# Sums of weights moved from GpSimd to VectorE, relu and square of h moved to ScalarE in two tiles, and one continued schedule

## The chip, the cores and the metric

The kernel runs on one core of a Trainium2 chip. The metric is the device time of that core in microseconds. Before the change the median of three runs is 893.88 us (890.68 to 894.46).

A core has five engines that run side by side, each through its own queue of instructions in order: TensorE (PE in the profile; PEld is its weight loads), VectorE (DVE), ScalarE (ACT), GpSimd (POOL) and SyncE (SP), which here issues nearly all DMAs. An instruction that waits holds back everything behind it on its engine.

## The reference

Attention without a softmax over scores, and then a two-layer network on its output:

```python
q_s = exp(q - max(q, axis=-1)); q_s /= sum(q_s, axis=-1) + 1e-9      # over the 64 features
k_s = exp(k - max(k, axis=2));  k_s /= sum(k_s, axis=2) + 1e-9       # over the 576 positions
kv  = einsum('bhsd,bhse->bhde', k_s, v)
x   = einsum('bhsd,bhde->bhse', q_s, kv)      # (8, 8, 576, 64) -> 4608 rows of 512
h   = maximum(x @ w_in, 0)                    # w_in 512 x 2048
out = (h * h) @ w_out                         # w_out 2048 x 512
```

q, k and v have 8 batches, 8 heads, 576 positions and 64 features, all in float32.

## The kernel before, in words

**Tiles.** A tile is the first 512 rows of one batch (t = 0 to 7), and a ninth tile holds the last 64 rows of all eight batches. While the network of tile t runs on PE, the attention of batch t + 1 runs beside it, in four pairs of heads; its result is the next tile's input `x`. The network goes by 16 blocks f of 128 hidden columns: `first` makes `h` of block f in a PSUM bank (two banks, tag "h", take turns) by 12 products, `split_g` turns it into its square, and `second` adds the square's products with w_out to four accumulators, for block f - 2. Each float32 operand is held as a high part and a rest (`gh` and `gl` for the square, `hi` and `lo` elsewhere), and three of the four cross products are taken.

**Relu and square.** ScalarE makes `r` = relu(h). For f under `ON_ACT` (14) VectorE then makes h = max(h, 0) * r in the bank itself (`scalar_tensor_tensor`), ScalarE makes `gh` = r squared, and VectorE `gl` = h - gh, which is the bank's last reader. For f from 14 on, in t = 1 and 2, ScalarE squares `r` in place, and the bank is free after the relu.

**Sums of weights.** Tiles t = 3 to 5 and the closing stage multiply by a Strassen-Winograd scheme: 7 products of half-size blocks take the place of 8, and they need sums of blocks of the weights (s1 to s4). `in_sums` prepares those of w_in in t = 1 and 2 (8 keys, in three steps), `full_sums`, `add_sums`, `split_sums`, `rest_sums` and `keep_sums` those of w_out in t = 3 to 6 (7 keys; an eighth is made in the closing stage). Each key adds the high parts and rests to full weights, makes four sums of 256 columns, has ScalarE copy them to a high part (`sums_h`), subtracts that from them in place, and sends both to memory. Before the change nearly all of this but the copy is GpSimd's; one of the two full additions of a w_in key is VectorE's. Buffers are few: pool `cvt` has two of tag "w", which the sums share with the output tiles `o`.

**GpSimd's other work.** From t = 1 on it is one `partition_all_reduce` for each pair of heads (`k_reduce`): the maximum of k over the 128 partitions, from `km` to `kmx`. The compiled program has a row ISA without operands where GpSimd goes over from ordinary additions to an all-reduce and one where it comes back.

**Order.** `Planner` sets the order of all engines at once. `Engine` gives each call a duration (`base + per * n` us, for VectorE 0.14 + 0.00108 * n, n being the columns), `order` places calls one after the other at the earliest free time of their engine, by the longest remaining chain (`tail`), and `plan.due` ties a call to a block of the network. The program has two plans: one for t = 0 (`plan.run`) and one for t = 1 to 5 (`plan.run_on`). Between them x is split and tile 0 is closed (`split_x`, `end_tile`, `prepare`) in the order of the code, and `reopen` then starts the second plan from an empty chip, every engine free at time zero. Tile 6 and the closing stage are in the order of the code. Nothing in the planner's durations stands for what GpSimd does between an addition and an all-reduce.

Of the kernel before, what the change touches and what calls it, by code (L numbers as in the profile page):

```python
# [132 lines left out]
class Planner:  # L133
# [9 lines left out]
    def __init__(self):  # L143
        self.open, self.nodes, self.into, self.chain, self.boot = True, [], None, None, []
        self.marks, self.line = {}, {}
        self.due, self.dues = None, []
        self.ease = 0.0
        self.locked, self.slack = False, 1.0

    def reopen(self, pools):  # L150

        for n in self.nodes:
            for b in n.buffers:
                b.seen, b.users, b.choices = [], [], ()
                b.last = b.before = b.placed = None
        for p in pools:
            p.told.clear()
        self.__init__()
        self.line, self.locked, self.slack, self.ISSUE = None, True, 1.06, 0.8

    def run_on(self):

# [122 lines left out]
            n.tail -= n.ease  # L285
    def order(self):

        left = {n: len(n.before) for n in self.nodes}
        for n in self.nodes:
            n.since, n.start, n.end = 0.0, None, None  # L290
            for b in n.buffers:
                b.placed = None
        ready = [n for n in self.nodes if not left[n]]
        free, dma, told, port = {}, self.FIRST, [], 0.0
        self.banks = {}
        while ready:
            able = []
            for n in ready:
                t = max(free.get(n.engine, 0.0), n.since)
                if self.locked and n.port:  # L300
                    t = max(t, port)
                if n.behind is not None:
                    if n.behind.start is None:
                        continue
                    t = max(t, n.behind.start + n.behind.busy)
                for b in n.buffers:
                    if b.placed is not None:
                        continue
                    at, _ = self.place(b)
                    if at is None:  # L310
                        break
                    t = max(t, at + self.HOP)
                else:
                    able.append((t, n))
            t0, n0 = min(able, key=lambda x: x[0])
            t, n = max(
                ((t, n) for t, n in able if n.engine is n0.engine and t <= t0 + self.WAIT),
                key=lambda x: x[1].tail,
            )
            n.start, n.end = t, t + n.busy  # L320
            free[n.engine] = n.end
            if n.port:
                port = n.end
            if n.moved:
                dma = max(dma, n.end) + n.moved / self.RATE
                n.end = dma + self.LAND
            for b in n.buffers:
                if b.placed is None:
                    b.placed = t
                    if b.choices:  # L330
                        b.pool, b.tag = self.place(b)[1]
                        self.banks[b.tag] = float("inf")
            for b in n.buffers:
                if b.choices and all(u.end is not None for u in b.users):
                    self.banks[b.tag] = max(u.end for u in b.users)
            told.append(n)
            ready.remove(n)
            for o in n.after:
                left[o] -= 1
                o.since = max(  # L340
                    o.since, n.end + (0.0 if o.engine is n.engine and not n.moved else self.HOP)
                )
                if not left[o]:
                    ready.append(o)
        return told

    def shift(self, seed):
# [23 lines left out]
def attention_ffn(  # L371
# [30 lines left out]
    C = 4  # L402
# [33 lines left out]
    WT = B - 1  # L436
    STRASSEN = range(3, WT - 1)
    DUE = 3
    ON_ACT = 14
    assert B * TL == M and DM == NP * P and C * P == M  # L440

    def pool(name, bufs, to=ctx, **more):
# [727 lines left out]
    def in_sums(j, i):  # L1170

        key = "in", j
        if i == 0:
            full = made["full", key] = cvt.tile([P, 2, M], F32, tag="w", name=f"full_i{j}")
            for k in range(2):
                slab = slabs[2 * j + k]
                (V if k else G).tensor_tensor(
                    out=full[:, k, :].only(k), in0=slab[:, 0, :], in1=slab[:, 1, :], op=ALU.add,
                    n=M if k else 575,
                )  # L1180
        elif i == 1:
            full = made.pop(("full", key))
# [8 lines left out]
            for out, in0, in1, op in (  # L1191
                (s1, a21, a22, ALU.add), (s2, s1, a11, ALU.subtract),
                (s3, a11, a21, ALU.subtract), (s4, a12, s2, ALU.subtract),
            ):
                G.tensor_tensor(out=out, in0=in0, in1=in1, op=op, n=260)
            hi = cvt.tile([P, 2, 2, HM], F32R, tag="w", name=f"sums_h_i{j}")
            for k in range(2):
                S.copy(out=hi[:, k].only(k), in_=two[k])
# [1 line left out]
        else:  # L1200
            hi, two = made.pop(("split", key))
            for k, (at, by) in enumerate(((4, 2), (8, 4))):
                to = w_sums[j][:, at:at + 2 * by, :].rearrange("p (n t) c -> p n t c", t=by)
                names = ("s2", "s1") if k == 0 else ("s3", "s4")
                lo = two[k].bitcast(F32R)
                G.tensor_tensor(out=lo, in0=two[k], in1=hi[:, k].only(k), op=ALU.subtract, n=575)
                for m, part in enumerate((hi[:, k].only(k), lo)):
                    Y.dma_start(
                        out=to[:, :, m, :].only(*((name, m) for name in names)),
                        in_=part.bitcast(F32), kb=256,  # L1210
                    )
# [106 lines left out]
    def store(t, acc, c):  # L1318
# [9 lines left out]
        if t == 0:  # L1328
            rows = rows.rearrange("(d a b c) e -> c d b a e", c=C, a=2, b=32)[c]
            for d in range(2):  # L1330
                Y.dma_start(out=rows[d], in_=o[d * HD:(d + 1) * HD, :])
        elif t < TB:
            rows = rows.rearrange("(h p k) e -> h k p e", h=2, k=2)[c % 2, c // 2]
            Y.dma_start(out=rows, in_=o, kb=256)
# [190 lines left out]
    def end_tile(t, parts, acc, one, two):  # L1525

        for c, f in (
            (0, one), (1, one), (0, two), (1, two), (2, one), (2, two), (3, one), (3, two),
        ):
            second(t, f, parts[f], acc, c, end=two)  # L1530
            if f == two:
                store(t, acc, c)

    KEYS = [("o", j) for j in range(PAIRS - 1)]
    IN_SUMS = [(j, i) for j in range(PAIRS) for i in range(3)]

    def sums_step(t, f):
# [5 lines left out]
                in_sums(*IN_SUMS.pop(0))  # L1543
        for key, at in SUMS_AT.get(t, ()):
            if f == at[0]:
                full_sums(key, 0, G)
            if f == at[1]:
                full_sums(key, 1, G)
            if f == at[2]:
                for n in range(3):  # L1550
                    add_sums(key, n, G)
            if f == at[3]:
                add_sums(key, 3, G)
                split_sums(key)
            if f == at[4]:
                rest_sums(key, G)
            if f == at[5]:
                keep_sums(key)

# [258 lines left out]
    for t in range(WT):  # L1818
        if t == 1:
            for i in range(NF):  # L1820
# [1 line left out]
                    whole[i] = whole[i].only((key, i, 0), (key, i, 1))  # L1822
                wi_h[i], wi_l[i] = (slabs[i][:, m, :].only(("i", i, m)) for m in range(2))
                wo_h[i], wo_l[i] = (slabs_o[i][:, m, :].only(("o", i, m)) for m in range(2))
            plan.reopen((const, att, cvt, ffn, tiny, boot, late, ps_o, ps_h, ps_a, dram))
        x_next = begin_next(t)
        if t in STRASSEN:
            acc = None
# [54 lines left out]
                ahead(f, x_next)  # L1883
        if t == 0:
            plan.run(SEEDS, fill)
            x = split_x(x_next, t + 1)
            end_tile(t, parts, acc, NF - 2, NF - 1)
            if todo[-1][1] == NF - 1 and t + 2 < B:
# [379 lines left out]
```

## Time and profile before

| | |
|---|---|
| median of three runs | 893.88 us (890.68 to 894.46) |
| profiled execution | 894.29 us, of it span 892.5 us |
| PE busy | 823.4 us (92% of the span), 4941 products |
| VectorE, ScalarE, GpSimd busy | 563.7, 451.3, 238.5 us |
| chain that ended last | PE 67%, DMA 12%, issue 9%, DVE 4%, POOL 3%, ACT 3% |
| mean granted TensorE clock | 0.973 |

PE is the engine with the most work, and its end is the kernel's. Stretches of the span used below: t = 1 from 133 to 237 us, t = 2 to 344, t = 3 to 5 to 641, t = 6 to 745, then the closing stage. To read the profile, ask of a stretch how long PE was idle, what released it, and at what clock it went on: a granted clock of 1.00 is 2.4 GHz, 0.50 is 1.2 GHz. The busy time of PE is not all useful time, since at the lower clock the same products count for longer. GpSimd's "issue" is idle time in which it waited for nothing that the profile shows.

### The profile page before, as it was taken

The numbers are of one execution on the slowest core, as the hardware profiler recorded it, in microseconds if no ns is written. First come the engines' busy times: TensorE is split into PE (matmuls) and PEld (weight loads), VectorE is DVE, ScalarE is ACT, GpSimd is POOL, SyncE is SP. The second block draws the span as 40 slices with busy tenths as digits, with TensorE's granted clock in tenths as the row PEclk, the third lists the DMA queues.
The fourth block names the chain that finished last, engine by engine and source line by source line (L and its number), as shares of the span: only waits on it lengthen the run. The fifth ranks groups of instructions, "written<-read, shape, count | busy, mean of one in ns | idle before, by whom it ended". The sixth has DMA issues, their size and how long they took to land.

```text
span 892.5 us, 14319 instructions
## 1 busy us (share of the span) xinstructions
PE 823.4 (92%) x4941; PEld 699.0 (78%) x4941; DVE 563.7 (63%) x1107; ACT 451.3 (51%) x864; POOL 238.5 (27%) x257
## 2 busy tenths in 40 slices
PE   8989998869997999898999799499998999999997
PEld 6678876748786877787888788388886888888886
DVE  6988976446583657465766566365675763327895
ACT  5888753233442335555666456255633344557452
POOL 4899953350024230412022302222021000000000
PEclk9999999989998999999999999799999999999999
DMA  9991126557232337986988779498944316999675
GB/s 282 385 338 39 48 49 177 162 178 216 56 109 62 107 105 206 262 259 189 250 250 243 217 211 287 133 259 241 275 122 118 86 39 226 377 374 343 231 204 95
DMA packets 224903, 174.28 MB, mean 195 GB/s; under 512 B 133568, under 2 KB 193472, under 8 KB 224832
## 3 DMA queue, kind: packets, MB, share of 16 engines
q1 hardware_dynamic: 218912, 171.67, 63.6%
q10 hardware_dynamic: 5920, 1.71, 0.8%
q8 instruction: 39, 0.64, 0.3%
q14 instruction: 32, 0.26, 0.1%
HBM read 129.37 MB, written 43.38 MB: 194 GB/s over the span
## 4 chain that ended last, share of the span: by engine, by line
PE 67%; DMA 12%; issue 9%; DVE 4%; POOL 3%; ACT 3%; SPq 2%; POOLq 0%; ACTq 0%; DVEq 0%
PE h L101 23%; PE acc L101 22%; PE out L2042 8%; PE h L1311 8%; PE kv L101 4%; DMA ring<-w_sums 3%; DMA bst<-bst 2%; SPq L101 2%; DMA q<-in_q_dram 2%; POOL sums_i L101 1%; DMA raw<-in_moe_w_out_dram 1%; DMA k<-in_k_dram 1%; DMA raw<-in_moe_w_in_dram 1%; DVE bst L101 1%; POOL sums_o L101 1%
## 5 line engine op out<-in xcount | busy, mean ns | idle before, releaser
L101 PE MATMUL acc<-w,gh 128*128 128x512 f32 x888 | 270.2, 386 | 2.7 <-DVE g L101 1.8
L101 PE MATMUL h<-x,w 128*128 128x512 f32 x768 | 190.0, 398 | 22.6 <-DVE gl L101 21.5
L101 PEld LDWEIGHTS h<-x,w 128*128 128x128 f32 x768 | 148.4, 197 | 53.6 <-DVE gl L101 24.6
L101 PEld LDWEIGHTS acc<-w,gh 128*128 128x128 f32 x888 | 159.9, 191 | 29.2 <-issue 6.7
L101 PE MATMUL acc<-w,gl 128*128 128x512 f32 x444 | 169.2, 381 | 0.7 <-DVE gl L101 0.7
L101 PEld LDWEIGHTS h<-w,ring 128*128 128x128 f32 x720 | 92.2, 192 | 24.5 <-ACT u L101 15.5
L101 PE MATMUL h<-w,ring 128*128 128x256 f32 x720 | 94.5, 278 | 17.4 <-ACT u L101 14.7
L101 POOL PARTITION_ALL_REDUCE kmx<-km x24 | 18.2, 760 | 289.7 <-DVE km L101 229.0
L101 PEld LDWEIGHTS acc<-w,gl 128*128 128x128 f32 x444 | 84.5, 190 | 14.0 <-DVE gl L101 1.9
L101 ACT ACTIVATE c<-c 128x512 f32<-128x512 f32 (+1 forms) x134 | 79.4, 592 | 19.1 <-DVE c L101 17.2
L2042 PE MATMUL out<-w,w 128*128 128x512 f32 x324 | 72.2, 379 | 0.0
L2042 PEld LDWEIGHTS out<-w,w 128*128 128x128 f32 x324 | 61.2, 189 | 8.8
L101 DVE TENSOR_TENSOR gl<-h,gh 128x512 fp32r<-128x512 f32 x59 | 40.4, 685 | 42.0 <-ACT gh L101 40.3
L101 ACT ACTIVATE r<-h 128x512 f32<-128x512 f32 x64 | 37.8, 590 | 47.0 <-PE h L101 47.0
L101 DVE SCALAR_TENSOR_TENSOR h<-h,r 128x512 f32<-128x512 f32 x60 | 41.5, 692 | 28.9 <-ACT r L101 28.6
L101 ACT ACTIVATE gh<-r 128x512 fp32r<-128x512 f32 x63 | 39.6, 629 | 39.5 <-PE acc L101 38.8
L101 ACT COPY u<-h 128x256 f32<-128x256 f32 x72 | 26.7, 371 | 52.3 <-PE h L101 52.0
L101 DVE TENSOR_REDUCE bst<-q 128x18 f32<-128x576 f32 x48 | 35.9, 748 | 25.9 <-DMA q<-in_q_dram 20.5
L101 DVE TENSOR_TENSOR c<-h,u 128x256 f32<-128x256 f32 x72 | 29.8, 418 | 34.3 <-ACT u L101 17.6
L101 PE MATMUL h<-w,w 128*128 128x256 f32 x288 | 39.5, 288 | 10.1 <-ACT u L101 6.8
L101 PEld LDWEIGHTS h<-w,w 128*128 128x128 f32 x288 | 37.8, 201 | 13.8 <-ACT u L101 8.2
L101 DVE TENSOR_TENSOR bst<-bst 128x18 f32<-128x18 f32 (+1 forms) x96 | 25.0, 260 | 33.6 <-DMA bst<-bst 18.6
(191 smaller groups left out, 1256.2 us busy)
## 6 DMA issues: line engine op xcount, KB each, us to landing
ring<-w_sums SPq DMA_DIRECT2D x24, 768.0 KB, 6.0
ring<-w_sums SPq DMA_DIRECT2D x64, 256.0 KB, 5.3
w<-w_sums SPq DMA_DIRECT2D x60, 256.0 KB, 5.2
w<-w_sums SPq DMA_DIRECT2D x24, 512.0 KB, 5.5
k<-in_k_dram SPq DMA_DIRECT2D x32, 256.0 KB, 3.4
raw<-in_moe_w_in_dram SPq DMA_DIRECT2D x16, 512.0 KB, 9.0
raw<-in_moe_w_out_dram SPq DMA_DIRECT2D x16, 512.0 KB, 9.5
w_sums<-w SPq DMA_DIRECT2D x32, 256.0 KB, 3.1
```

The source lines that it names most:

```text
L101: getattr(self.eng, op)(*map(real, args), **{k: real(a) for k, a in kwargs.items()})
L1311: nc.tensor.matmul(out=out.real(), lhsT=a[:, k * P:(k + 1) * P].real(), rhs=in_turn(m[k]).real(), start=(begin and k == 0 and i == 0), sto ...
L2042: nc.tensor.matmul(out=banks[name][m].real(), lhsT=a[:, m * P:(m + 1) * P].real(), rhs=in_turn(b[:, i, :]).real(), start=fresh and j == i ...
```

## The change

Three things are changed. `in_sums` and the output sums in `sums_step` run wholly on VectorE. `ON_ACT` goes from 14 to 0, so in t = 1 and 2 ScalarE makes relu and both squares for every block. And `reopen` is replaced by `go_on`, called right behind the first plan: the second plan keeps the state in which the first ended (when each engine and the DMA are free, which buffers are held), and it also holds the split of x and the close of tile 0. The closing stage calls the same functions with VectorE as before.

```diff
-    def reopen(self, pools):
-        for n in self.nodes:
-            for b in n.buffers:
-                b.seen, b.users, b.choices = [], [], ()
-                b.last = b.before = b.placed = None
-        for p in pools:
-            p.told.clear()
-        self.__init__()
-        self.line, self.locked, self.slack, self.ISSUE = None, True, 1.06, 0.8
+        self.past, self.state = [], ({}, self.FIRST, 0.0, {})
+
+    def go_on(self):
+        self.past += self.nodes
+        self.state = self.reached
+        self.open, self.nodes, self.into = True, [], None
+        self.marks, self.dues = {}, []
+        self.locked, self.slack, self.ISSUE = True, 1.06, 0.8
...
-        free, dma, told, port = {}, self.FIRST, [], 0.0
-        self.banks = {}
+        (free, dma, port, self.banks), told = self.state, []
+        free, self.banks = dict(free), dict(self.banks)
...
-    ON_ACT = 14
+    ON_ACT = 0
...
-                (V if k else G).tensor_tensor(
-                    out=full[:, k, :].only(k), in0=slab[:, 0, :], in1=slab[:, 1, :], op=ALU.add,
-                    n=M if k else 575,
+                V.tensor_tensor(
+                    out=full[:, k, :].only(k), in0=slab[:, 0, :], in1=slab[:, 1, :], op=ALU.add
                 )
...
-                G.tensor_tensor(out=out, in0=in0, in1=in1, op=op, n=260)
+                V.tensor_tensor(out=out, in0=in0, in1=in1, op=op, n=HM)
...
-                G.tensor_tensor(out=lo, in0=two[k], in1=hi[:, k].only(k), op=ALU.subtract, n=575)
+                V.tensor_tensor(out=lo, in0=two[k], in1=hi[:, k].only(k), op=ALU.subtract)
...
             if f == two:
+                plan.due = (t + 1) * NF + 1
                 store(t, acc, c)
+                plan.due = None
...
             if f == at[0]:
-                full_sums(key, 0, G)
+                full_sums(key, 0)
             if f == at[1]:
-                full_sums(key, 1, G)
+                full_sums(key, 1)
             if f == at[2]:
                 for n in range(3):
-                    add_sums(key, n, G)
+                    add_sums(key, n)
             if f == at[3]:
-                add_sums(key, 3, G)
+                add_sums(key, 3)
                 split_sums(key)
             if f == at[4]:
-                rest_sums(key, G)
+                rest_sums(key)
...
-            plan.reopen((const, att, cvt, ffn, tiny, boot, late, ps_o, ps_h, ps_a, dram))
...
             plan.run(SEEDS, fill)
+            for c in range(C):
+                ps_o.told.setdefault(f"o{c}", []).append(acc[c].buffer)
+            plan.go_on()
             x = split_x(x_next, t + 1)
```

On GpSimd, around the second all-reduce of t = 1 (before): `sums_i` and `full_i` are sums of w_in, `km` and `kmx` the maximum of k, and a row ISA without operands stands at each change of kind.

```order
L101 ISA
L101 ISA kmx_1_1781<-km_1_1723 128x128
L101 ISA
L101 TENSOR_TENSOR sums_i_0_1839<-full_i_1731 128x256
L101 TENSOR_TENSOR sums_i_0_1839<-sums_i_0_1839,full_i_1731 128x256
L101 TENSOR_TENSOR sums_i_1_1851<-full_i_1731 128x256
L101 TENSOR_TENSOR sums_i_1_1851<-full_i_1731,sums_i_0_1839 128x256
L101 TENSOR_TENSOR sums_i_0_1839<-sums_i_0_1839,sums_h_i_1863 128x512
L101 TENSOR_TENSOR sums_i_1_1851<-sums_i_1_1851,sums_h_i_1863 128x512
L101 TENSOR_TENSOR full_i_1902<-w_710 128x512
L101 ISA
L101 ISA kmx_2_1938<-km_2_1886 128x128
```

On the same engine now, from the last addition of tile 0 on:

```order
L101 TENSOR_TENSOR w_1563<-w_1444,w_1563 128x512 x2
L101 ISA
L101 ISA kmx_0_1685<-km_0_1658 128x128
L101 ISA kmx_1_1861<-km_1_1832 128x128
L101 ISA kmx_2_1998<-km_2_1950 128x128
L101 ISA kmx_3_2198<-km_3_2170 128x128
L101 ISA kmx_0_2497<-km_0_2288 128x128
```

The additions have left; the 24 all-reduces stand one behind the other, with one ISA row ahead of the first.

On ScalarE, around the second key of w_in in t = 1 (before): `r` and `gh` are relu and square of block 4 and 5, `sums_h_i` the copy of the sums, and `q` an exponential of the attention.

```order
L101 ACTIVATE r_4_1857<-h_4_1823 128x512
L101 CAST sums_h_i_1863<-sums_i_0_1839 128x512
L101 CAST sums_h_i_1863<-sums_i_1_1851 128x512
L101 ACTIVATE gh_4_1883<-r_4_1857 128x512
L101 ACTIVATE q_1_1807<-q_1_1807 128x576
L101 ACTIVATE r_5_1914<-h_5_1879 128x512
L101 ACTIVATE gh_5_1931<-r_5_1914 128x512
```

On ScalarE now, around the same key:

```order
L101 ACTIVATE r_5_1887<-h_5_1857 128x512
L101 ACTIVATE kt_1526<-kt_1526 64x128
L101 ACTIVATE q_1_1827<-q_1_1827 128x576
L101 ACTIVATE gh_5_1914<-r_5_1887 128x512
L101 ACTIVATE r_5_1887<-r_5_1887 128x512
L101 CAST sums_h_i_1929<-sums_i_0_1916 128x512
L101 ACTIVATE r_6_1942<-h_6_1909 128x512
L101 CAST sums_h_i_1929<-sums_i_1_1924 128x512
L101 ACTIVATE gh_6_1965<-r_6_1942 128x512
L101 ACTIVATE r_6_1942<-r_6_1942 128x512
```

The copies still stand between a relu and its square, but they now wait for VectorE; each block has one more square.

On VectorE now, around the same key: `gl` is the rest of the square of blocks 5 and 6, `km` the maximum of k within a partition.

```order
L101 TENSOR_TENSOR sums_i_0_1916<-full_i_1845 128x256
L101 TENSOR_TENSOR sums_i_0_1916<-sums_i_0_1916,full_i_1845 128x256
L101 TENSOR_TENSOR sums_i_1_1924<-full_i_1845 128x256
L101 TENSOR_TENSOR gl_5_1932<-r_5_1887,gh_5_1914 128x512
L101 TENSOR_TENSOR sums_i_1_1924<-full_i_1845,sums_i_0_1916 128x256
L101 TENSOR_TENSOR sums_i_0_1916<-sums_i_0_1916,sums_h_i_1929 128x512
L101 TENSOR_REDUCE km_2_1950<-k_2_1889 128x128
```

The sums' additions stand among the rests `gl`, where before the products h = max(h, 0) * r stood; the third of them reuses a buffer whose contents a DMA takes to memory.

## Rows read from the trace of the kernel before

**Rows 1.** Busy time by stretch: busy us and count per engine, granted clock, DMA share, GB/s.

```profile
133.00:237.00 104.00, 87.71 (x459) 71.18 (x458) 55.66 (x114) 32.61 (x66) 29.59 (x32) 0.93 0.56 166
237.00:344.00 107.00, 99.64 (x543) 80.67 (x541) 65.45 (x135) 41.63 (x83) 32.38 (x33) 0.97 0.36 96
344.00:641.00 297.00, 268.08 (x1972) 237.97 (x1970) 179.61 (x401) 165.08 (x362) 60.60 (x60) 0.97 0.82 237
641.00:745.00 104.00, 100.96 (x551) 84.84 (x551) 67.41 (x132) 39.95 (x79) 11.50 (x12) 0.97 0.34 96
```

**Rows 2.** Timeline of PE: start, duration, operation, count, idle time before it and releaser.

```profile
148.04 4.54 PE L101 MATMUL h<-x,w 128*128 128x512 f32 x12 [3.57 <-DVE gl L101]
...
169.03 4.54 PE L101 MATMUL h<-x,w 128*128 128x512 f32 x12 [3.50 <-DVE gl L101]
...
176.00 2.75 PE L101 MATMUL h<-x,w 128*128 128x512 f32 x12
...
189.89 4.45 PE L101 MATMUL h<-x,w 128*128 128x512 f32 x12 [8.54 <-DVE gl L101]
...
286.10 1.54 PE L101 MATMUL kv<-qT,kv 64*64 64x64 f32 x8 [4.95 <-ACT kv L101]
...
319.74 2.86 PE L101 MATMUL h<-x,w 128*128 128x512 f32 x12 [2.19 <-DVE gl L101]
...
412.67 0.94 PE L101 MATMUL h<-w,ring 128*128 128x256 f32 x6 [1.53 <-ACT u L101]
...
507.14 2.92 PE L101 MATMUL h<-w,w 128*128 128x256 f32 x12 [4.94 <-ACT u L101]
...
511.52 1.50 PE L101 MATMUL h<-w,ring 128*128 128x256 f32 x12
...
576.67 1.65 PE L101 MATMUL h<-w,ring 128*128 128x256 f32 x6 [13.15 <-ACT u L101]
...
688.68 5.49 PE L101 MATMUL h<-x,w 128*128 128x512 f32 x12 [3.02 <-DVE gl L101]
```

**Rows 3.** Busy time by stretch, as in Rows 1, behind two of these gaps.

```profile
286.10:294.10 8.00, 8.00 (x37) 4.33 (x38) 2.00 (x8) 2.33 (x7) 2.41 (x2) 0.62 0.76 194
576.70:583.70 7.00, 7.00 (x29) 6.35 (x30) 4.72 (x8) 3.32 (x8) 2.22 (x2) 0.60 0.58 187
```

**Rows 4.** Timeline of all engines ahead of the gap that ends at 189.89.

```profile
185.05 0.71 POOL L101 TENSOR_TENSOR sums_i<-full_i 128x256 f32<-128x256 f32 x1 [6.87 <-issue]
...
186.59 0.62 ACT L101 CAST sums_h_i<-sums_i 128x512 fp32r<-128x512 f32 x1 [12.38 <-POOL sums_i L101]
...
188.48 0.62 ACT L101 ACTIVATE gh<-r 128x512 fp32r<-128x512 f32 x1
...
189.14 0.69 DVE L101 TENSOR_TENSOR gl<-h,gh 128x512 fp32r<-128x512 f32 x1 [10.24 <-ACT gh L101]
```

**Rows 5.** Timeline, an all-reduce that follows an all-reduce on GpSimd.

```profile
249.54 0.28 DVE L101 TENSOR_TENSOR km<-km,kt 64x128 f32<-64x128 f32 x1
250.00 0.70 POOL L101 PARTITION_ALL_REDUCE kmx<-km  x1 [9.70 <-DVE km L101]
```

**Rows 6.** Groups of instructions: busy us, mean ns of one, idle before.

```profile
L101 DVE TENSOR_TENSOR sums_o<-sums_o,sums_h_o 128x512 fp32r<-128x512 f32 x2 | 1.3, 682 | 0.0
L101 DVE TENSOR_TENSOR sums_o<-full_o 128x256 f32<-128x256 f32 x2 | 0.8, 416 | 0.0
L101 DVE SCALAR_TENSOR_TENSOR h<-h,r 128x512 f32<-128x512 f32 x60 | 41.5, 692 | 28.9 <-ACT r L101 28.6
L101 ACT ACT_TABLE_LOAD x1 | 1.3, 1283 | 3.2 <-issue 3.2
```

**Rows 7.** Timeline of GpSimd, a sum that waits for its buffer.

```profile
294.38 0.73 POOL L101 TENSOR_TENSOR sums_i<-full_i 128x256 f32<-128x256 f32 x1 [5.87 <-DMA w_sums<-sums_i]
```

**Rows 8.** What PE waited for: us in total, times, longest.

```profile
PE h L101 <- DMA ring<-w_sums: 2.8, 2, 1.5
PE h L101 <- DVE c L101: 2.0, 2, 1.1
```

More of the change, by code (lines that the diff above doesn't have):

```diff
@@ L286, in order @@
     def order(self):
-        left = {n: len(n.before) for n in self.nodes}
         for n in self.nodes:
-            n.since, n.start, n.end = 0.0, None, None
+            n.start = n.end = None
             for b in n.buffers:
-                b.placed = None
+                if b.users[0].end is None:
+                    b.placed = None
+        left = {n: sum(o.end is None for o in n.before) for n in self.nodes}
+        for n in self.nodes:
+            n.since = max((o.end + self.HOP for o in n.before if o.end is not None), default=0.0)
         ready = [n for n in self.nodes if not left[n]]
-        free, dma, told, port = {}, self.FIRST, [], 0.0
-        self.banks = {}
+        (free, dma, port, self.banks), told = self.state, []
+        free, self.banks = dict(free), dict(self.banks)
         while ready:
@@ L344, in order @@
                     ready.append(o)
+        self.reached = free, dma, port, self.banks
         return told
@@ L1330, in store @@
             for d in range(2):
-                Y.dma_start(out=rows[d], in_=o[d * HD:(d + 1) * HD, :])
+                Y.dma_start(out=rows[d], in_=o[d * HD:(d + 1) * HD, :], kb=128)
         elif t < TB:
```

## The prediction

> **What bounds the kernel now.** I read first the busy times by stretch, to see how much of each stretch PE did not work and at what clock it did; then PE's timeline, for each idle time and what ended it; then, for one of them, the timeline of all engines, to follow the wait back to where it begins.
>
> In t = 1 PE is busy for 87.7 of 104 us at a mean clock of 0.93, in t = 3 to 5 for 268 of 297 at 0.97 [rows 1]. So PE sets the time, and it loses some of it in two ways: it waits, and behind a wait it goes on at 1.2 GHz. Twelve products with 512 columns take 2.75 us at full clock, but 4.54 behind the gaps at 148 and 169 us [rows 2].
>
> The waits are few and long. The nine in [rows 2] are 3.57, 3.50, 8.54, 4.95, 2.19, 1.53, 4.94, 13.15 and 3.02, together 45.4 us. They name VectorE (`gl`) or ScalarE (`u`, `kv`) as releaser, but neither is where the time goes. Follow the one of 8.54 us back [rows 4]: PE waits for `gl` on VectorE, which had been idle for 10.24 us until ScalarE made `gh`; ScalarE had been idle for 12.38 us, since ahead of `gh` in its queue stood the copy of the sums of weights, which waits for GpSimd; and GpSimd stood still for 6.87 us between an all-reduce and its first addition, waiting for nothing that the profile shows ("issue"). This is the cost of going over from one kind of GpSimd work to the other, which the planner's durations do not hold: it put the copy where it believed the sums to be ready. The other eight gaps end the same way, ScalarE's queue held by a copy of sums that waits for GpSimd.
>
> That the going over costs, and not the all-reduce itself, is seen where one all-reduce follows another: `km` ends at 249.82 and the reduction starts at 250.00 [rows 5].
>
> The Trainium skill says the same of one direction (GPSIMD Engine Reference, section 2.1 Instruction dispatch): the first call into freshly loaded code on GpSimd pays about 6 us that no instruction in the profile shows. The trace agrees with the size, 6.87 us, but shows it on the way back to plain additions too [rows 4]. By the rule alone a return would be free, and gaps as this one would have another cause and stay; the sum below goes by the rows.
>
> **The change part by part.**
>
> *The waits that go.* With the sums on VectorE, GpSimd has nothing but all-reduces from t = 1 on, and goes over once ahead of the first, where tile 0's last products still run. All nine waits lose their cause: 45.4 us. What comes next in their place is the copy's wait for VectorE, which does a key's additions between its own other work.
>
> *The clock behind them.* From the rows' own durations against 2.75 us for twelve products of 512 columns and 1.50 for twelve of 256 [rows 2]: 1.79 + 1.79 + 1.70 (at 148, 169, 190), 1.42 (at 507), 2.74 (at 689), together 9.4 us. Behind the gaps at 286 and 577 the forms change, so I take the granted clock: in a stretch without idle time the loss is its length times one less the clock, 8.0 x 0.38 + 7.0 x 0.40 = 5.8 us [rows 3]. Together 15.3 us, as long as no new wait takes the clock down.
>
> *VectorE's new work.* A key of w_in adds one full addition (0.68), four additions of 256 columns (0.42 each) and two rests (0.68 each): 3.7 us. A key of w_out adds a second full one: 4.4 us [rows 6]. That is 8 x 3.7 + 7 x 4.4 = 60 us. In t = 1 and 2 it loses 28 products h = max(h, 0) * r of 0.69 us, 19 us [rows 6]. So it gains 5 us in each of t = 1 and 2 and 9 us in each of t = 3 to 5. It has room: in t = 1 it would be busy for 61 us of what is left of 104 (83), in t = 3 to 5 for 206 of 273, 75% instead of 60% [rows 1]. It is not the bound, but it hides less. PE's waits for `c` there are 2.0 us now [rows 8]; between nothing and the whole 26 us of new work in t = 3 to 5, I take 3 us, by the row.
>
> *ScalarE's new work.* 28 squares of 0.62 us [rows 4], 17 us on 74 in 211 [rows 1]: hidden behind PE. `gl` comes a square later, but the bank of `h` is now free after the relu and no longer after `gl`, so PE need not wait for `gl` before the next block: priced at nothing; were this cover gone, it would cost the 0.62 us of a block 28 times, 17 us. The Trainium skill has a rule against such an edit (ScalarE: Activation LUTs, section What ACT_TABLE_LOAD costs): a switch to another set of functions costs about 2.66 us, so 28 squares among exponentials could cost 28 x 2 x 2.66 = 149 us, an estimate by that page. The trace shows one load in the whole program, though squares and exponentials already alternate on ScalarE [rows 6]; by the row it is nothing.
>
> *DMA.* The bytes stay. In t = 3 to 5 the queues are busy for 0.82 of 297 us, 243 us [rows 1]; the gaps there give back 19.6 us and their clock 4.2, so the same transfers must fit into 273 us, 0.89. PE's waits for weights (`ring`) are 2.8 us now [rows 8]. At best they stay, at worst the stretch keeps its share of 0.82 and all 24 us are lost again. I take 4 us, nearest to the row.
>
> *Waits that move to VectorE.* A sum that reuses a buffer must wait until a DMA has taken its contents away. One such wait on GpSimd was 5.87 us [rows 7]. Now it would stand in VectorE's queue, ahead of `gl`, and PE waits for `gl`. The planner counts a transfer's time, and VectorE is free a quarter of the time; the bounds are nothing and 15 keys of 5.87 us, 88 us. I take 2 us, since one row out of many shows such a wait at this length.
>
> *The joint schedule.* At the end of tile 0 VectorE now takes the first reduction of the next q ahead of the split of x. PE still has the closing products of tile 0 then, so I price it at nothing; without that cover it would be one VectorE instruction, under 1 us, either way. The all-reduces and SP's queue keep their order around it.
>
> *Sum.* 894.3 (the profiled execution) - 45.4 - 15.3 + 3 + 4 + 2 = 842.6, so 843 us. The profiled execution is 0.4 us above the median, which changes nothing.
>
> **The rivals.**
>
> *More comes back (834 us).* If VectorE's room and the queues hide everything, nothing is added: 833.6 us. For it speaks that the planner's duration for a VectorE instruction on 512 columns (0.14 + 0.00108 x 512 = 0.69 us) is the measured one, so that its order should hold, and that gaps smaller than the nine may share their cause; against it the DMA share.
>
> *DMA takes it back in t = 3 to 5 (863 us).* The stretch stays as long as its transfers need at the share of today: 842.6 - 4 + 24. For it speaks 0.82 over 297 us; against it that PE's waits for `ring` are two in the whole program [rows 8].
>
> *GpSimd pays again without going over (867 us).* If an all-reduce behind an all-reduce needed the 6.87 us too, VectorE, whose next instruction waits for `kmx`, would stand still 24 times for longer than the 5.5 us of PE's work on one block (2.75 for its products and as much for the accumulators): 24 x 1.4 = 33 us on 833.6. Against it speaks [rows 5]. This is also the case that the change doesn't do what it says.
>
> *Slower (922 us): VectorE takes over GpSimd's buffer waits.* At each of the 15 keys VectorE waits for a DMA as GpSimd did at 294 us, and PE behind it: 833.6 + 88. It decides from 60.7 / 15 = 4.0 us per key on. For it speaks that the queue is in order and that the buffers are few (two of tag "w" for sums and output tiles); against it that GpSimd had such a wait of this length once, and that the planner keeps VectorE on other work meanwhile.
>
> **How the numbers follow.** My forecast 0.58, more comes back 0.20, DMA 0.13, GpSimd again 0.03, slower 0.06. About 0.5% is what a measurement of this kernel can tell from no change, so 889 to 898 us counts as the same. Three of the four rivals are on the fast side: faster 0.94; of the slow one a third would come out near its point of decision: same 0.02, slower 0.04. The range runs from 830 (smaller gaps gone too) to 863 (the DMA case); 0.09 of the chances lie above it, and some of the forecast's and the first rival's own spread below.
>
> **What would show it.** Right: GpSimd's idle times before an all-reduce end with `km`, no "issue" of some 7 us from t = 1 on; ScalarE's copies of sums wait for VectorE, under 2 us; no PE wait of over 3 us between 130 and 745 us; a granted clock of 1.00 in t = 1 and 2; t = 1 in about 83 us, t = 3 to 5 in about 280. Wrong: PE waits that end with `gl` or `c` behind a VectorE idle time that a DMA ends (the slow case), a share of the queues near 0.9 with waits for `ring` of several us (the DMA case), or a gap before each all-reduce.

## The result and the profile after

The kernel after takes 835.73 us (median of four runs, 834.26 to 836.20), the kernel before, on the same chip beside it, 892.28 us (median of four). The ratio is 0.9375, with a 95% interval of 0.932 to 0.943: 6.2% faster, where 843 us were predicted. The profiled execution took 834.26 us, of it span 832.4, 60.1 less than the span before.

The span falls in two ways, which the page gives without looking at any wait. PE's idle time (span less busy) goes from 69.1 to 22.9 us, 46.2 less; PE's busy time goes from 823.4 to 809.5, 13.9 less for the same 4941 products, since fewer of them ran at 1.2 GHz. The prediction's two large terms were 45.4 and 15.3.

By stretch, in the order t = 1, t = 2, t = 3 to 5, t = 6, closing stage (columns as in [rows 1]; the ends are put, as near as the new order allows, at the same products of PE as before):

```profile
133.30:216.50 83.20, 83.20 (x474) 68.62 (x473) 57.59 (x133) 41.99 (x82) 5.33 (x5) 1.00 0.66 198
216.50:311.00 94.50, 94.27 (x527) 78.44 (x526) 67.21 (x147) 50.63 (x98) 3.11 (x4) 1.00 0.41 110
311.00:582.00 271.00, 265.27 (x1974) 235.67 (x1972) 196.38 (x446) 164.30 (x359) 9.73 (x12) 0.99 0.87 256
582.00:685.50 103.50, 99.98 (x550) 83.98 (x551) 67.59 (x139) 40.18 (x80) 3.60 (x4) 0.98 0.37 105
685.50:832.40 146.90, 142.08 (x658) 123.81 (x656) 87.14 (x119) 76.12 (x117) 0.00 (x0) 1.00 0.84 279
```

Read the first two numbers of a row against each other: in t = 1 PE now has no idle time at all, and the clock is 1.00. Against [rows 1] the stretches are 20.8, 12.5, 26.0 and 0.5 us shorter; t = 6 has given back nothing. The products in t = 1 and t = 2 differ from [rows 1] by 15 more and 16 fewer, since their order has changed, so these two are best taken together: 33.3 us. GpSimd's share is down to 5.33 us in t = 1, and VectorE works 196 of 271 us in t = 3 to 5.

The idle times of PE of over 0.8 us between 133 us and the end:

```profile
312.48 1.60 PE L101 MATMUL h<-w,ring 128*128 128x256 f32 x12 [0.88 <-DMA ring<-w_sums]
333.26 0.80 PE L101 MATMUL acc<-w,gl 128*128 128x512 f32 x1 [3.35 <-DVE gl L101]
605.68 4.54 PE L101 MATMUL h<-x,w 128*128 128x512 f32 x12 [3.15 <-DVE gl L101]
```

There are three, where the kernel before had sixteen: the nine in [rows 2] and seven more of 0.93 to 1.51 us. None stands at a place of the nine; the first stands where one of the seven stood, at the first products of t = 3 (1.51 us before, at 345.86). The row at 605.68 also shows the price behind a wait that is known from [rows 2]: 4.54 us for twelve products where 2.75 are needed.

The second key of w_in, which [rows 4] showed as a stall (GpSimd 6.87, ScalarE 12.38, VectorE 10.24 us), on ScalarE and VectorE now:

```profile
159.68 0.42 DVE L101 TENSOR_TENSOR sums_i<-full_i 128x256 f32<-128x256 f32 x1
160.45 0.60 ACT L101 CAST sums_h_i<-sums_i 128x512 fp32r<-128x512 f32 x1
160.58 0.69 DVE L101 TENSOR_TENSOR gl<-r,gh 128x512 fp32r<-128x512 f32 x1 [0.48 <-ACT r L101]
161.19 0.42 DVE L101 TENSOR_TENSOR sums_i<-full_i,sums_i 128x256 f32<-128x256 f32 x1
162.49 0.61 ACT L101 CAST sums_h_i<-sums_i 128x512 fp32r<-128x512 f32 x1
```

Neither copy has an idle time before it; the one wait in the five rows is 0.48 us. All the copies together waited 76.2 us for GpSimd before, and wait once now, 2.42 us.

GpSimd from tile 0's last addition on, which answers to [rows 5]:

```profile
125.59 2.50 POOL L101 TENSOR_TENSOR w<-w,w 128x512 fp32r<-128x512 f32 x2 [2.24 <-ACT w L101]
136.21 0.72 POOL L101 PARTITION_ALL_REDUCE kmx<-km  x1 [8.12 <-DVE v L101]
152.30 1.67 POOL L101 PARTITION_ALL_REDUCE kmx<-km  x1 [15.36 <-DVE km L101]
164.47 1.12 POOL L101 PARTITION_ALL_REDUCE kmx<-km  x1 [10.50 <-DVE km L101]
```

Every idle time ends with an input, none with "issue". The one going over that is left lies in the 8.12 us ahead of the first all-reduce, beside PE's work.

What PE waited for, against [rows 8]:

```profile
PE acc L101 <- DVE gl L101: 4.3, 4, 3.3
PE h L101 <- DVE gl L101: 3.2, 1, 3.2
PE h L101 <- DMA ring<-w_sums: 0.9, 1, 0.9
```

The wait for `c` is gone, that for `ring` fell from 2.8 to 0.9 us. All waits of PE together are 18.1 us, where they were 63.9.

The gap at 333.26 is the rival "VectorE takes over GpSimd's buffer waits", once. On VectorE:

```profile
329.86 1.29 DVE L101 TENSOR_TENSOR full_o<-w 128x512 f32<-128x512 f32 x2 [5.18 <-DMA out_dram<-o]
331.07 0.74 DVE L101 TENSOR_REDUCE bst<-q 128x18 f32<-128x576 f32 x1
331.85 0.76 DVE L101 TENSOR_TENSOR q<-q,bst 128x576 f32<-128x576 f32 x1
332.52 0.68 DVE L101 TENSOR_TENSOR gl<-c,gh 128x512 fp32r<-128x512 f32 x1
```

The first addition of a key shares its buffers with the output tiles, waits 5.18 us until tile 2's output has left, and `gl` stands three places behind it. The gap at 605.68 is no wait for a sum: VectorE waits 4.72 us for the transfer of `q` (at 600.35), and in t = 6, where relu and square have kept their old form, the bank of `h` is held until `gl`. Before, the same reduction waited 1.36 us for `q` (at 656.14). SyncE issues that transfer behind others. PE's first products of t = 6 and the last issue of `q` behind them, now:

```profile
586.82 7.50 PE L101 MATMUL h<-x,w 128*128 128x512 f32 x34
...
594.77 2.59 SPq L101 DMA_DIRECT2D q<-in_q_dram  x3
```

and before:

```profile
645.97 4.26 PE L101 MATMUL h<-x,w 128*128 128x512 f32 x19
...
649.90 3.25 SPq L101 DMA_DIRECT2D q<-in_q_dram  x4
```

The last of the four leaves 10.5 us behind the first product now (597.36 less 586.82), where it was 7.2 (653.15 less 645.97). What SyncE waits for in that stretch has changed too. From 585 to 600 us it now waits for earlier transfers of weights:

```profile
SPq L101 <- DMA w<-w_sums: 2.0, 3, 1.4
```

Before, from 644 to 656 us, it had no such wait, but 2.3 us of waits for VectorE and ScalarE. Why `q` leaves later was not tested.

### The profile page after: what moved, and what is told of

It is laid out like the page before. It is cut to its first block, busy times and chain, and to the rows that moved or that the text cites. A ratio compares the mean times of both kernels' runs of the same rounds, so it can differ in the third digit from the quotient of the medians.

```text
span 832.4 us, 14246 instructions
## 1 busy us (share of the span) xinstructions
PE 809.5 (97%) x4941; PEld 691.3 (83%) x4941; DVE 584.5 (70%) x1191; ACT 468.6 (56%) x892; POOL 126.2 (15%) x145
## 4 chain that ended last, share of the span: by engine, by line
PE 83%; DMA 8%; DVE 3%; ACT 2%; SPq 2%; issue 1%; POOL 0%; DVEq 0%; POOLq 0%; ACTq 0%
PE acc L101 31%; PE h L101 29%; PE out L2047 9%; PE h L1312 9%; PE kv L101 5%; SPq L101 2%; DMA k<-in_k_dram 2%; DMA w<-w_sums 2%; DMA raw<-in_moe_w_out_dram 1%; DMA raw<-in_moe_w_in_dram 1%; DVE bst L101 1%; DMA out_dram<-o 1%; PE x L101 1%; DMA ring<-w_sums 1%; DVE gl L101 0%
## 5 line engine op out<-in xcount | busy, mean ns | idle before, releaser
L101 PE MATMUL h<-x,w 128*128 128x512 f32 x768 | 181.6, 386 | 4.2 <-DVE gl L101 3.2
L101 PEld LDWEIGHTS h<-x,w 128*128 128x128 f32 x768 | 144.0, 190 | 30.7 <-issue 4.2
L101 POOL PARTITION_ALL_REDUCE kmx<-km x24 | 20.3, 845 | 492.9 <-DVE km L101 439.1
L101 ACT ACTIVATE c<-c 128x512 f32<-128x512 f32 (+1 forms) x134 | 79.4, 592 | 16.1 <-DVE c L101 13.7
L101 DVE TENSOR_TENSOR c<-h,x_joint 128x512 f32<-128x512 f32 x24 | 16.6, 690 | 44.2 <-ACT x_joint L101 27.6
L101 DVE TENSOR_REDUCE bst<-q 128x18 f32<-128x576 f32 x48 | 35.9, 748 | 16.3 <-DMA q<-in_q_dram 10.5
L101 POOL TENSOR_TENSOR w<-w,w 128x512 fp32r<-128x512 f32 x32 | 41.2, 1299 | 4.4 <-ACT w L101 4.2
L101 POOL TENSOR_TENSOR w<-w,raw 128x512 int32<-128x512 int32 x32 | 41.4, 1305 | 1.0 <-issue 0.3
L101 ACT ACTIVATE q<-q 128x576 f32<-128x576 f32 (+1 forms) x32 | 21.4, 669 | 32.4 <-DVE q L101 31.4
```

Source lines behind the costliest of these rows:

```text
L101: getattr(self.eng, op)(*map(real, args), **{k: real(a) for k, a in kwargs.items()})
```

## The experiments

**Which part of the change is it?** Four kernels: the sums alone, ScalarE's part alone, the schedule alone, and the whole without the sums. In two of the texts below, tiles are counted from one: "tiles 2 and 3" are t = 1 and 2, and "the schedule of tile 2" is that of t = 1.

```diff
# sums alone, on the kernel before (and reversed, on the kernel after, for the fourth)
-                G.tensor_tensor(out=out, in0=in0, in1=in1, op=op, n=260)
+                V.tensor_tensor(out=out, in0=in0, in1=in1, op=op, n=HM)
...
# ScalarE's part alone
-    ON_ACT = 14
+    ON_ACT = 0
...
# schedule alone (one line of it)
-            plan.reopen((const, att, cvt, ffn, tiny, boot, late, ps_o, ps_h, ps_a, dram))
+            plan.go_on()
```

> The kernel before, with nothing changed but the engine of the sums: all on VectorE. Relu and square of h stay as they were, and so do the rules of the schedule. Theory (GpSimd's going over between additions and all-reduces held ScalarE's copies of sums, and these held PE): this alone brings nearly the whole change, 834 to 846 us, and no PE wait of over 4 us is left from t = 1 on. Rival 'the bank of h, freed by ScalarE, is what helps': little is gained here, 875 to 892 us. Rival 'the schedule': the same, 875 to 892 us.

> The kernel before with relu and square of h on ScalarE in tiles 2 and 3 from the first block on; sums and schedule as before. Theory: the nine waits stay (their cause is GpSimd), 880 to 896 us. Rival 'the bank of h': most of the 56 us come back, 836 to 855 us.

> The kernel before with nothing but the schedule of tile 2 going on from that of tile 1; sums on GpSimd and VectorE as before. Theory: the planner still counts nothing for going over, so the waits stay, if at other places: 880 to 900 us. Rival 'the schedule': 836 to 860 us.

> The kernel after with the sums back on GpSimd; ScalarE's relu and square of h and the joint schedule stay. Theory: the waits return, 875 to 900 us, with stretches of 5 to 8 us on GpSimd that wait for nothing the profile shows, and PE waits behind them. Rivals 'the bank of h' and 'the schedule' (either or both together): 836 to 855 us.

| kernel | median us | ratio to before, 95% | copies of sums waited, us | PE waited, us |
|---|---|---|---|---|
| before (the profile above) | 893.88 | | 76.2 | 63.9 |
| sums alone | 839.27 | 0.940 (0.937 to 0.943) | 6.1 | 21.2 |
| ScalarE's part alone | 895.62 | 1.004 (1.001 to 1.007) | 78.7 | 64.0 |
| schedule alone | 902.05 | 1.012 (1.010 to 1.015) | 65.8 | 65.4 |
| after, sums back on GpSimd | 904.85 | 1.013 (1.009 to 1.017) | 63.3 | 66.7 |
| after | 835.73 | 0.938 (0.932 to 0.943) | 2.4 | 18.1 |

Each ratio is to runs of the kernel before beside it on the same chip (median 891.91 us for the four in the middle). The sums alone are the gain, within the measurement. Both rivals are refuted: without the sums the other two parts bring nothing, and the schedule alone costs 1.2%. "No PE wait of over 4 us" holds too (the longest is 2.9). The last two came out 2 and 5 us above the ranges written for them: with the sums on GpSimd the new order moves the waits to other places. They are 10 and 13 us slower than before, and in the traces most of that is clock: PE waits hardly longer, but its busy time is 829.3 and 832.7 us where it was 823.4. Why was not settled.

**Is it the going over, or that GpSimd adds slowly?** Two kernels leave the additions where they are and take the going over away; one leaves it and tells the planner.

```diff
# no all-reduce: on the kernel before, and on the kernel after with the sums back on GpSimd
-        G.partition_all_reduce(kmx, km, channels=P, reduce_op=RED.max, n=300)
+        G.tensor_copy(out=kmx, in_=km, n=300)
...
# the planner knows: in order(), on the kernel before
+                if n.kind is not None and kind is not None and n.kind != kind and self.locked:
+                    t += 6.9
```

> The kernel before, sums on GpSimd as they were, but each all-reduce of km across partitions replaced by a plain GpSimd copy km to kmx, at the same place of the same order (this leaves out the maximum over the partitions). GpSimd then does one kind of work only and has no going over. Theory: the waits go although GpSimd still does the additions, 838 to 855 us, and no stretch of 5 us and more on GpSimd that waits for nothing. Rival 'GpSimd is slower at additions than VectorE' (1.27 us against 0.68) or 'two engines' queues instead of one': the waits stay, 875 to 895 us.

> The kernel after with the sums back on GpSimd, and each all-reduce of km replaced by a plain copy km to kmx at the same place (this leaves out the maximum over the partitions). Against the same kernel with the all-reduces (904.85 us) only the going over is gone. Theory: 828 to 840 us, no PE wait of over 4 us, and idle times on GpSimd that end with a copy of sums, km or a DMA, but hardly any of some 7 us that wait for nothing. Rival 'additions on GpSimd are too slow or too late for ScalarE's queue': 870 us and more.

> The kernel before, the engines of all work as before, but the planner of the written-out order counts 6.9 us whenever GpSimd changes between additions and all-reduces, so that it places ScalarE's copies and PE's work with this in view. Theory: the price stays on GpSimd but fewer waits reach PE; 845 to 880 us. Rival 'GpSimd's time itself is short, not its order': 885 to 900 us.

The kernel before without all-reduces takes 832.07 us (ratio 0.935, 0.931 to 0.939), with every addition still on GpSimd: as fast as the kernel after. So it was not the additions' speed. What GpSimd waited for in this kernel is not shown here; the trace of the next one shows it. On the kernel after with the sums back, the same edit takes 904.85 to 852.45 us (0.957 of before, 0.951 to 0.962): 52 of 69 us. GpSimd there has one idle time that waits for nothing the profile shows, of 3.91 us, and none of some 7 us. But the time is not within the 828 to 840 expected, and there is a PE wait of 4.90 us against "none over 4". That wait is not a going over. Its GpSimd, ScalarE and PE rows:

```profile
334.24 2.52 POOL L101 TENSOR_TENSOR full_o<-w 128x512 f32<-128x512 f32 x2 [9.39 <-DMA out_dram<-o]
...
340.16 1.14 ACT L101 CAST sums_h_o<-sums_o 128x512 fp32r<-128x512 f32 x2 [7.12 <-POOL sums_o L101]
...
342.19 2.93 PE L101 MATMUL h<-w,w 128*128 128x256 f32 x12 [4.90 <-ACT u L101]
```

It is the same buffer, shared with the same output tile, that made VectorE wait at 329.86 in the kernel after. This accounts for 5 us of the 17 by which it stays above after; the rest is not broken down.

With the price in the planner the kernel takes 853.16 us (0.959, 0.955 to 0.963), inside its range: GpSimd now changes its kind 21 times from t = 1 on where it did 35 times, the copies wait 18.2 us instead of 76.2, and PE 27.7 instead of 63.9. No engine's work was changed. So 36 us (889.32 beside it, less 853.16) of the 56 come back by nothing but an order made with the price in it. That order has both fewer changes and fewer waits behind each; what each of the two is worth was not separated.

**What exactly goes over?** On the kernel after, where GpSimd has no sums, one small instruction ahead of each all-reduce of t up to 5 is to bring the going over back: first a copy, then an addition.

```diff
         G.partition_all_reduce(kmx, km, channels=P, reduce_op=RED.max, n=300)
+        if plan.open:
+            plan.last.calls.insert(0, lambda: nc.gpsimd.tensor_copy(out=kmx.real(), in_=km.real()))
...
# then, in the copy's place
+            plan.last.calls.insert(0, lambda: nc.gpsimd.tensor_tensor(out=kmx.real(), in0=km.real(), in1=km.real(), op=ALU.add))
```

> The kernel after, with one plain GpSimd copy (km to kmx, written over at once) ahead of each of 20 all-reduces of t up to 5, in the same order otherwise. This brings the going over back at each all-reduce, though GpSimd has no sums. Theory: kmx comes some 7 us later 20 times, and VectorE's queue and then PE wait for it: 1.4 to 6 us each, 860 to 950 us. Rival 'going over is not what cost, the sums' additions on GpSimd were': 834 to 842 us.

> As the kernel with a plain copy ahead of each all-reduce, but with an addition (km + km to kmx, written over at once) in the copy's place, since the copy brought no going over. Theory: additions and all-reduces are the two kinds between which GpSimd goes over; each of 20 all-reduces then starts 6 to 7 us later, seen as idle time on GpSimd that waits for nothing, and VectorE, whose next step needs kmx, hands 1.4 to 6 us of it on to PE: 855 to 950 us. Rival 'going over costs only where a copy of sums stands behind it': the idle times show on GpSimd but not on PE, 834 to 848 us. Rival 'no going over for this addition either': 834 to 845 us without idle times.

The trace has 21 of each, not 20. With the copy the kernel takes 842.28 us, 0.947 (0.942 to 0.952) of before, so neither text had it right: it is below the theory's 860, and the rival's reason isn't it either, as the addition further down shows. The trace says why:

```profile
135.66 0.29 POOL L820 COPY kmx<-km 128x128 f32<-128x128 f32 x1 [8.04 <-DVE v L101]
142.95 0.72 POOL L101 PARTITION_ALL_REDUCE kmx<-km  x1 [7.00 <-issue]
157.45 1.29 POOL L820 COPY kmx<-km 128x128 f32<-128x128 f32 x1 [13.78 <-DVE km L101]
158.85 0.71 POOL L101 PARTITION_ALL_REDUCE kmx<-km  x1
169.55 0.81 POOL L820 COPY kmx<-km 128x128 f32<-128x128 f32 x1 [10.00 <-DVE km L101]
170.45 0.73 POOL L101 PARTITION_ALL_REDUCE kmx<-km  x1
```

The first all-reduce behind tile 0's additions pays 7.00 us, and from then on a copy between two all-reduces costs GpSimd its own time and nothing else. A copy does not go over. (By what way the 6.5 us over the kernel after come was not followed.) An addition does, each time:

```profile
155.92 1.38 POOL L820 TENSOR_TENSOR kmx<-km 128x128 f32<-128x128 f32 x1 [13.82 <-DVE km L101]
163.43 0.72 POOL L101 PARTITION_ALL_REDUCE kmx<-km  x1 [6.13 <-issue]
172.89 0.89 POOL L820 TENSOR_TENSOR kmx<-km 128x128 f32<-128x128 f32 x1 [8.74 <-DVE km L101]
181.23 0.72 POOL L101 PARTITION_ALL_REDUCE kmx<-km  x1 [7.45 <-issue]
```

927.48 us, 1.041 (1.037 to 1.045) times the kernel before, although GpSimd has next to nothing to do: 85 us more than with the copy, 4.1 for each. All 21 all-reduces behind an addition have an idle time that waits for nothing, 5.78 to 7.93 us, 144.2 in all. The way to PE is another than before. The copies of sums wait only 16.1 us; VectorE's next step needs `kmx` and waits in front of everything else:

```profile
DVE k L101 <- POOL kmx L101: 113.2, 20, 8.5
```

One case of it, on GpSimd, VectorE, ScalarE and PE:

```profile
472.44 0.72 POOL L101 PARTITION_ALL_REDUCE kmx<-km  x1 [7.87 <-issue]
...
473.20 0.69 DVE L101 TENSOR_TENSOR k<-k,kmx 128x512 f32<-128x512 f32 x1 [8.06 <-POOL kmx L101]
...
473.92 0.63 ACT L101 ACTIVATE ek<-k 128x512 f32<-128x512 f32 x1 [8.43 <-DVE k L101]
474.46 0.35 ACT L101 COPY u<-h 128x256 f32<-128x256 f32 x1
...
474.87 1.65 PE L101 MATMUL h<-w,w 128*128 128x256 f32 x6 [6.07 <-ACT u L101]
```

`ek` belongs to the attention of the next tile and could wait; but it stands ahead of `u`, which empties PE's bank.

**A better version.** Two kernels go for the two gaps that are left, beside the kernel after run once more.

```diff
-        if 0 < t < STRASSEN[0] and f >= ON_ACT:
+        if (0 < t < STRASSEN[0] or t == WT - 1) and f >= ON_ACT:
...
# and, in the second of them, the first key's blocks
-    TWICE = (4, 4, 5, 6, 8, 8), (9, 10, 12, 13, 14, 14)
+    TWICE = (5, 5, 6, 7, 8, 8), (9, 10, 12, 13, 14, 14)
```

> The kernel after, unchanged, as the measure for the runs beside it: 833 to 838 us.

> The kernel after, with relu and square of h on ScalarE in tile t = 6 too. Theory: the gap of 4.54 us at 605.68 (3.15 of it a wait for gl) goes, since the bank of h is then free after the relu and no longer after gl, and with it some 1.8 us of half clock behind it: 830 to 833 us. Rival 'gl itself is late, for VectorE waits for q': the accumulators wait for it instead, 834 to 838 us.

> The kernel with ScalarE's relu and square in t = 6, and the first key of the sums of w_out a block later. Theory: the gap at 333.26 goes as well (3.35 us behind an addition on VectorE that waits for an output tile's DMA, and some 1.7 us of half clock): 826 to 830 us. Rival: the additions wait elsewhere, or the weights come later, 831 to 838 us.

837.24, 836.44 and 837.84 us; against before 0.939, 0.940 and 0.940, all three with intervals of some 0.936 to 0.943: no difference, and both times lie in the ranges of the rivals. The first edit does what it was to do, the gap at 605.68 is gone, but smaller ones stand elsewhere, as at 469.54 (1.39), 557.21 (1.34), 618.54 (1.18) and 650.38 (1.24), and PE's waits add up to 21.3 us, as in the kernel beside it (22.2). The second edit failed at its own place:

```profile
329.01 1.29 DVE L101 TENSOR_TENSOR full_o<-w 128x512 f32<-128x512 f32 x2 [6.18 <-DMA out_dram<-o]
```

The addition still comes at 329 us, too early: in the code the block number says what has to follow the addition and not how early the planner may put it. PE's wait behind it is 4.35 us, and a new one of 4.16 us for a transfer of weights (`w<-w_sums`) stands at 559.88. So whether a later first key would help was not shown. No version faster than the kernel after was found that computes the same.

## Why the prediction was right, point by point

**The waits that go (45.4 us): right in cause, and near in size partly by luck.** All nine are gone. That the cause is GpSimd's going over and not its work is shown from three sides: without all-reduces the loss is gone though GpSimd still adds (832.07), with the price in the plan most of it is (853.16), and with the going over put back without sums it returns by another way (927.48). But the 46.2 us by which PE's idle time fell are a balance. The waits outside the nine, which the sum left out, went from 18.5 us (63.9 less 45.4) to 11.6 (18.1 less 3.35 and 3.15), 6.9 less, and the two new ones took 6.5.

**"The other eight gaps end the same way": seven do.** The one of 2.19 us at 319.74 goes back to a going over by another queue. GpSimd stood still ahead of the rests of sums; SyncE, which had issued nothing since 301.99, waited for these rests in order to send them to memory; the transfer of `k` stood behind them; and VectorE waited for `k` with `gl` next in its queue:

```profile
311.50 2.75 POOL L101 TENSOR_TENSOR sums_i<-sums_i,sums_h_i 128x512 fp32r<-128x512 f32 x2 [6.90 <-issue]
313.03 1.97 SPq L101 DMA_DIRECT2D w_sums<-sums_i  x2
315.09 0.42 SPq L101 DMA_DIRECT2D k<-in_k_dram  x1
318.04 1.05 DVE L101 TENSOR_REDUCE km<-k 128x128 f32<-128x512 f32 x1 [6.17 <-DMA k<-in_k_dram]
319.01 0.68 DVE L101 TENSOR_TENSOR gl<-h,gh 128x512 fp32r<-128x512 f32 x1
```

In the whole program SyncE waited 72.0 us for sums and their copies before, and 13.6 us after. The prediction has no term for this path. Which of the smaller waits went by it is not shown.

**The clock behind them (15.3 us): right in kind, 2 us too small.** PE's busy time fell by 13.9 although the two new gaps took some back, 1.79 at 605.68 and about 1.7 at 333 (below). Without these it would be 17.4.

**The charges (3 + 4 + 2 us): right in sum, wrong in each place.** VectorE's new work cost nothing that shows: it is busy 57.6 us in t = 1 (61 worked out) and 72% of t = 3 to 5 (75%), and PE's waits for `c`, the row by which 3 us were taken, are gone. The weights' transfers in t = 3 to 5 cost nothing: their share rose to 0.87 of 271 us, near the 0.89 feared, but PE's waits for `ring` fell. Buffer waits on VectorE were priced at 2 us over all keys; one came, and it is 3.35 us with the clock down to 0.66 behind it:

```profile
333.00:338.00 5.00, 4.74 (x20) 4.30 (x21) 2.91 (x11) 2.50 (x7) 0.00 (x0) 0.66 0.17 42
```

that is 3.35 and about 1.7 (5.00 x 0.34), 5 us. Another 5 us came in t = 6 by a transfer (next point). So the new costs are 10 us, where 9 were charged, and it is not the charges that put the forecast 8 us above the profiled execution (842.6 and 834.26). The gains were larger than worked out: 6.9 us of smaller waits and 2 us of clock. By stretch, t = 3 to 5 is 26.0 us shorter with the new wait of 5 in it, where 23.8 were worked out (19.6 and 4.2); t = 1 and 2 together are 33.3 shorter, where some 31 were.

**The rival "more comes back" (834 us) had the time, but half of the reason.** It charged nothing, and 10 us came. Its other reason, that smaller gaps share the cause, fits the 6.9 us, but these gaps were not followed back one by one. That these nearly cancel is luck.

**"No PE wait of over 3 us between 130 and 745": wrong, twice.** Beside the one at 333.26 there is that of t = 6, and with it t = 6 stayed at 103.5 us, where the wait at 688.68 and its clock, 5.8 us, should have come back. The cause is a transfer after all: `q` leaves SyncE 3.3 us later against PE's work than before, as the two pairs of rows above show. SyncE waited 2.0 us for transfers of weights there, so these may have a part in it. The charge for DMA, 4 us, thus came to 4.9 us (3.15 and 1.79), but in a stretch where none was looked for. The other signs came as told: no "issue" on GpSimd, a clock of 1.00 in t = 1 and 2, t = 1 in 83.2 us; t = 3 to 5 took 271 instead of 280, and one copy of sums waited 2.42 us, over the 2 allowed.

**ScalarE's part and the joint schedule (nothing): right** as far as can be told: with the sums moved, 839.27 with neither and 835.73 or 837.24 with both, in overlapping intervals. The trace after has one table load on ScalarE, as before, so the 149 us that the prediction estimated for such loads did not come.

**The rival "GpSimd pays again" had the right mechanism and a price too low.** It put 1.4 us on each all-reduce that goes over, by letting a whole block of PE's work (5.5 us) cover it. The run with the additions measured 4.1. Of these 2.5 are PE's waits (76.9 us, against 24.2 with the copy, over 21) and 1.3 its lower clock (busy 840.2 us, against 813.1), which the rival did not price. And a block of work did not cover 5.5 us: in the case shown above 6.07 of the 7.87 us reached PE, because ScalarE's `u` stood behind `ek`.

**What one going over costs: right.** The rule of the Trainium skill (GPSIMD Engine Reference, section 2.1 Instruction dispatch: the first call into freshly loaded code costs about 6 us that no instruction shows) agrees in size, 6.13 to 7.45 us in the rows above; that code is loaded there no run shows. These runs add that it is paid at each change between an addition and an all-reduce, both ways, and not between a copy and an all-reduce. So a return is not free, as the prediction took it to be by the rule alone: the 6.87 us in [rows 4] are one. A wait for an input can hide it, as in the 8.12 us ahead of the first all-reduce after.

## What to carry to other kernels

An engine that looks a quarter busy can still set the end if it changes between two kinds of work: look for idle time that ends with "issue", follow it through each in-order queue to the bound engine, and either give the engine one kind of work or put the price into whatever makes the order. The same price hit PE through ScalarE in one kernel and through VectorE in another, so ask of each late result what is queued behind the instruction that takes it, not only who needs it. When such stalls go, waits too small for a list go with them, and new small ones come where buffers and queues are shared: here 9 us came back that the sum did not have, and 10 us were lost in places where it did not look, or not for so much.

## What had not been expected

VectorE's busy time rose by 20.8 us only, though its instructions add 60 and lose 19. Its small instructions on two inputs became shorter: the mean of `bst<-bst` on 36 columns fell from 290 to 195 ns, of the one on 18 columns with a scalar from 291 to 178. In the kernel after with the sums back and no all-reduces the first is 261 ns, in the one with GpSimd's copies ahead of the all-reduces 195, so the sums on GpSimd do it. The three forms of `bst<-bst` that became shorter make up 9.7 of the 20 us. In the kernel before, the same instruction beside an idle GpSimd and beside an addition:

```profile
151.03 0.18 DVE L101 SCALAR_TENSOR_TENSOR bst<-bst 128x18 f32<-128x18 f32 x1
...
192.51 0.72 POOL L101 TENSOR_TENSOR sums_i<-full_i 128x256 f32<-128x256 f32 x1 [0.79 <-DVE bst L101]
192.52 0.75 DVE L101 SCALAR_TENSOR_TENSOR bst<-bst 128x18 f32<-128x18 f32 x1
```

0.18 us alone, 0.75 where it begins with GpSimd's 0.72: it ends when the addition does. The Trainium skill has this (SBUF — State Buffer, section Who interferes with whom): a VectorE instruction with two inputs in SBUF contends with a GpSimd instruction that reads SBUF; the ports that the two share are an exclusive lock, and the order of issue decides who is blocked. The trace agrees, also in that the reductions `bst<-q`, with one input, take 748 ns in both kernels. Moving the sums thus gave VectorE some of their time back, which the sum had not counted. It is not what the change gains: the kernel before without all-reduces (832.07 us) still has every addition on GpSimd.
